# A searched issue order kept as a table, with semaphores between VectorE and GpSimd

## The chip, the cores and the metric

The kernel runs on one core of a Trainium2 chip. The metric is the device time in microseconds (us) of one execution. Most times below are medians of all executions of a kernel; an execution counts as slow when it lies over 1.5% above the fastest of the same kernel, and the ratios and their intervals use the fast ones alone. The span in a profile is the time from the first to the last instruction, 1.7 us less than the metric (190.1 of 191.84 us before).

Engines in the profile: PE is TensorE's matmuls, PEld its weight loads, DVE is VectorE, ACT is ScalarE, POOL is GpSimd, SP is SyncE. Each engine gets its own list of instructions. In the kernel before, ScalarE (198 operations), VectorE (184) and GpSimd (31) start their instructions in the order of the list, so one that waits holds up all that stand behind it; the ScalarE lines further down show a copy of 0.78 us held up by a logarithm that waits 2.11 us for its load.

## The reference

A gated linear attention over 4 batches, 8 heads, 768 steps and head size 48, then an MLP mixer over its output.

```python
# attention
for t in range(S):
    state = alpha[:, :, t, :, None] * state + np.einsum('bhd,bhe->bhde', k[:, :, t], v[:, :, t])
    y[:, :, t] = np.einsum('bhd,bhde->bhe', q[:, :, t], state)
# x = y as (4, 768, 384); token mixing, then channel mixing
h  = np.maximum(x.transpose(0, 2, 1) @ w_tok1, 0.0) @ w_tok2
u  = x + h.transpose(0, 2, 1)
h2 = np.maximum(u @ w_ch1, 0.0) @ w_ch2
out = u + h2
```

## The kernel before

The attention is done in 12 chunks, three to a batch (n = 0 to 11). One chunk takes four loads (`at`, `kt`, `qt`, `vt`, 384 KB each), logarithms and exponentials on ScalarE, elementwise products on VectorE or GpSimd (`pkk`, `pkq`), and small matmuls on parts of the 128x128 array (64*128, 48*128, 64*64 and 48*64 in the trace). The mixer of a batch then has large matmuls of 128x384: token mixing (`t1`, `t2`), transposes (`up`), channel mixing (`c1`, 72 matmuls in 24 groups, each group followed by a relu `rt`; `c2`, 72 matmuls in 24 groups), output adds (`o`) and stores (`st`). Attention of later chunks is laid between the mixer's matmuls of earlier batches.

The program is a list of 838 operations with predecessors, costs and buffer classes. A scheduler written in Python runs while the kernel is being built. It picks the next operation greedily by a cost model and a priority, chooses the engine where there is a choice, and the order that comes out is the order in which each engine gets its instructions:

```python
    def once(self):
        ...
        while avail:
            ...
            for o in avail:
                ...
                for e, (occ, lat) in o.eng.items():          # engines that could do it
                    st = free[e] if free[e] > r else r
                    if e == "PE":
                        ...
                        if o.mode != mode:                   # other array shape
                            st += 95.0
                    elif o.port and port_by != e and port > st and (e == "DVE" or e == "POOL"):
                        st = port                            # model: other engine still in one marked port
                    c = (st, o.pr, st + lat, o, e, occ, lat)
                    if own is None or c[2] < own[2]:
                        own = c                              # earliest finish
                ...                                          # then: earliest start, priority
```

A relu may run on ScalarE or VectorE, and earliest finish sends nearly all of them to ScalarE. A fence (`fe`, a copy of four columns whose result nobody reads; the second half waits for it) on ScalarE or VectorE stands between the two halves `ia` and `ib` of one chunk's attention output:

```python
            ho = ... either(act(384), dve(384)) ...          # relus
        ia = O("ia", pe([48] * 4), 15, ..., mode="R")
        fe = O("fe", either(act(4), dve(4)), 15, reads=[yp], preds=[ia], ...)
        io = O("ib", pe([48] * 4), 15, ..., preds=[fe], mode="R")
```

Both halves of every output tile are stored from SyncE's queue, which also issues all input loads:

```python
    def store(self, o, b, i):
        dst = self.out[b, i * 128 : (i + 1) * 128, :].rearrange("(t s) d -> s t d", s=2)
        for h in range(2):
            self.nc.sync.dma_start(dst[h], self.t(o)[64 * h : 64 * h + 64, :])
```

Of the kernel before, what the change touches and what calls it, by code (L numbers as in the profile page):

```python
# [13 lines left out]
SEM = 50.0  # L14


class Val:
    __slots__ = ("cls", "ops", "buf", "name")

    def __init__(self, cls, name=""):  # L20
        self.cls, self.ops, self.buf, self.name = cls, [], None, name


class Op:
    __slots__ = ("name", "eng", "prio", "preds", "vals", "emit", "mode", "idx",
                 "start", "end", "on", "dma", "port", "pr", "occ", "rdy")

    def __init__(self, name, eng, prio, vals, preds, emit, mode=None, dma=None):
        self.name, self.eng, self.prio = name, eng, prio
        self.vals, self.preds, self.emit = vals, preds, emit  # L30
        self.mode, self.dma = mode, dma
        self.start = self.end = None
        self.on = None
# [31 lines left out]
class Plan:  # L65


    def __init__(self, classes):
        self.classes = dict(classes)
        self.ops = []  # L70
        self.shift = {}
        self.wint = []
# [4 lines left out]
    def op(self, name, eng, prio, writes=(), reads=(), preds=(), emit=None, mode=None, dma=None, port=False):  # L77
        vals = list(writes) + [v for v in reads if v not in writes]
        o = Op(name, eng, prio, vals, list(preds), emit, mode, dma)
        o.port = port  # L80
        for v in vals:
            v.ops.append(o)
        o.idx = len(self.ops)
        self.ops.append(o)
        return o

    def landed(self, s, need):

        t = s
        for a, b in self.wint:  # L90
# [14 lines left out]
    def run(self):  # L105
        self.wint = []
        for _ in range(3):
            self.once()
            w = []
            for a, b in sorted(self.wnew):  # L110
                if w and a <= w[-1][1] + 1.0:
                    w[-1] = (w[-1][0], max(b, w[-1][1]))
                else:
                    w.append((a, b))
            if w == self.wint:
                break
            self.wint = w
        return self.order

    def once(self):  # L120
        free = {e: 700.0 for e in ("PE", "ACT", "DVE", "POOL", "SP")}
        free["POOL"] = free["DVE"] = 3200.0
# [3 lines left out]
        HELD = 1e12  # L126
        bank = [0.0] * 8
        mode = None
        self.wnew = []
        dma_free, dma_w = 2400.0, 0.0  # L130
        warm, wi, acc = False, 0, 0.0
        order, npred, succ, nleft = [], {}, {}, {}
        for o in self.ops:
            o.start = o.end = o.on = None
            o.pr = o.prio + self.shift.get(o.name, 0.0)
            ps = set(o.preds)
            npred[o] = len(ps)
            for p in ps:
                succ.setdefault(p, []).append(o)
            for v in o.vals:  # L140
                nleft[v] = nleft.get(v, 0) + 1
                v.buf = None
        avail = [o for o in self.ops if npred[o] == 0]
        for o in avail:
            o.rdy = 0.0
        relt = {}
        while avail:
            t1 = min(bank)
            t2 = min(max(bank[i], bank[i + 1]) for i in range(0, 8, 2))
            best = None  # L150
            for o in avail:
                r = o.rdy
                for v in o.vals:
                    if v.buf is None:
                        c = v.cls
                        if c == "one":
                            t = t1
                        elif c == "pair":
                            t = t2
                        elif bufs[c]:  # L160
                            t = bufs[c][0][0]
                        else:
                            t = HELD
                        if t > r:
                            r = t
                if r >= HELD:
                    continue
                own = None
                for e, (occ, lat) in o.eng.items():
                    st = free[e] if free[e] > r else r  # L170
                    if e == "PE":
                        if not warm:
                            occ, lat = 2 * occ, 1.5 * lat
                        if o.mode != mode:
                            st += 95.0
                    elif o.port and port_by != e and port > st and (e == "DVE" or e == "POOL"):
                        st = port
                    c = (st, o.pr, st + lat, o, e, occ, lat)
                    if own is None or c[2] < own[2]:
                        own = c  # L180
                if best is None:
                    best = own
                elif own[4] == best[4]:
                    slack = 150.0 if own[4] == "PE" else 60.0
                    if own[1] < best[1]:
                        if own[0] <= best[0] + slack:
                            best = own
                    elif own[0] + slack < best[0] or (own[0] < best[0] and own[1] == best[1]):
                        best = own
                elif own[0] < best[0]:  # L190
                    best = own
            if best is None:
                raise RuntimeError("plan deadlock: " + ", ".join(o.name for o in avail[:30]))
            st, _, _, o, e, occ, lat = best
            o.start, o.on = st, e
            free[e] = st + occ
            self.busy[e] += occ
            o.end = st + lat + SEM
            o.occ = occ
            if o.port and e in ("DVE", "POOL"):  # L200
                port, port_by = st + (lat - 60.0 if e == "DVE" else occ), e
            if e == "PE":
                mode = o.mode
# [11 lines left out]
            if o.dma is not None:  # L215
                kind, dur, lead, tail = o.dma
                if kind == "w":
                    s = max(st + lead, dma_w)
                    dma_w = s + dur
                    self.wnew.append((s, dma_w))  # L220
                    o.end = dma_w + tail
                else:
                    dma_free = self.landed(max(st + lead, dma_free), dur)
                    o.end = dma_free + tail
            for v in o.vals:
                c = v.cls
                if v.buf is None:
                    if c == "one":
                        lim = max(t1, st - 200.0)
                        v.buf = max((i for i in range(8) if bank[i] <= lim), key=lambda i: (bank[i ^ 1], bank[i], -i))  # L230
                        bank[v.buf] = HELD
                    elif c == "pair":
                        lim = max(t2, st - 200.0)
                        v.buf = max((i for i in range(0, 8, 2) if max(bank[i], bank[i + 1]) <= lim),
                                    key=lambda i: (max(bank[i], bank[i + 1]), -i))
                        bank[v.buf] = bank[v.buf + 1] = HELD
                    else:
                        v.buf = bufs[c].pop(0)[1]
                nleft[v] -= 1
                relt[v] = max(relt.get(v, 0.0), o.end)  # L240
                if nleft[v] == 0:
                    if c == "one":
                        bank[v.buf] = relt[v]
                    elif c == "pair":
                        bank[v.buf] = bank[v.buf + 1] = relt[v]
                    else:
                        bufs[c].append((relt[v], v.buf))
                        bufs[c].sort()
            order.append(o)
            avail.remove(o)  # L250
            for s in succ.get(o, ()):
                npred[s] -= 1
                if npred[s] == 0:
                    s.rdy = max(p.end for p in s.preds)
                    avail.append(s)
        if len(order) != len(self.ops):
            raise RuntimeError("not scheduled")
        self.order = sorted(order, key=lambda o: o.start)
        self.span = max(o.end for o in order)


W_SHARE = 0.19
B, H, S, D = 4, 8, 768, 48
HD, DT, DCH = 384, 256, 1536
NB = 3
NS, NM, NDT, NDC = 6, 3, 2, 12
IN_NS, OUT_NS = 1215.0, 560.0
# [11 lines left out]
def build(g):  # L279
# [109 lines left out]
    def weight(nm, piece, npart, bytes_, gate, prio, stage=None):  # L389
        o = P.op(f"ldw_{nm}{piece}", {"POOL": (900.0, 900.0)}, prio, preds=[gate] if gate else [],  # L390
                 writes=[stage] if stage else [], emit=lambda e: g.weight(nm, piece, gate, stage), dma=("w", bytes_ / 285.0, 1600.0, 800.0))
# [3 lines left out]
    def mixer(b):  # L395
# [4 lines left out]
        for m in range(NDT):  # L400
            bank, ht = V("one"), V("ht")
            if b == 0:
                prev = None
                for kc in range(NS):
                    o = P.op(f"t1_{b}_{m}_{kc}", pe([384]), m0 + 900 * m * sc + kc, writes=[bank], reads=[x[kc][0]],
                             preds=[x[kc][1], wl[("wt1", 0)]] + ([prev] if prev else []),
                             emit=lambda e, m=m, kc=kc, bank=bank: g.tok1(bank, m, kc, x[kc][0]))
                    prev = o
            else:
                prev = P.op(f"t1_{b}_{m}", pe([384] * 6), m0 + 900 * m * sc, writes=[bank], reads=[v for v, _ in x],  # L410
                            preds=[o for _, o in x] + [wl[("wt1", 0)]],
# [36 lines left out]
        for i in range(NS):  # L448
# [3 lines left out]
            for q4 in range(4):  # L452
                pp = []
                for mc in range(3 * q4, 3 * q4 + 3):
# [8 lines left out]
            P.op(f"st_{b}_{i}", {"SP": (350.0, 350.0)}, m0 + (16800 + 1950 * (i + 1)) * sc + hold, reads=[o_], preds=[oo],  # L463
                 emit=lambda e, i=i, o_=o_: g.store(o_, b, i), dma=("i", OUT_NS, 1000.0, 700.0))
# [3 lines left out]
    weight("wt1", 0, 1, 786432, gates[NB - 1]["qt"], -70000.0)  # L468
    stage = V("ut")
    weight("wt2", 0, 1, 786432, gates[NB - 1]["qt"], -69990.0, stage)  # L470
# [385 lines left out]
```

## Time and profile before

Median 192.38 us over 3 runs (192.04 to 192.41); span of the profiled run 190.1 us.

Busy times in stretches of the span: each row gives the stretch and its length, then for PE, PEld, DVE, ACT and POOL in this order the busy us and, in brackets, the instructions; then the granted TensorE clock (1 is full; the first event recorded for it in this trace is at 30.4 us, and for the time ahead of that the row prints 1.00 although 128x384 matmuls start 320 ns apart there, twice the 162 of later; whether an event is missing, or the row has no state before the first one, is not shown), the DMA share and GB/s.

```profile
0.00:5.20 5.20, 0.00 (x0) 0.10 (x1) 1.77 (x13) 2.12 (x2) 2.33 (x12) 1.00 0.65 170
5.20:40.90 35.70, 25.01 (x589) 17.65 (x589) 28.01 (x42) 18.34 (x34) 13.20 (x14) 1.00 1.17 248
...
70.00:91.00 21.00, 16.90 (x206) 9.84 (x205) 14.76 (x25) 12.12 (x27) 7.88 (x7) 1.00 0.98 265
91.00:120.00 29.00, 29.00 (x464) 17.78 (x464) 16.80 (x29) 13.69 (x30) 0.42 (x1) 1.00 0.17 40
...
185.10:190.10 5.00, 0.01 (x1) 0.00 (x0) 0.61 (x2) 0.00 (x0) 0.00 (x0) 0.73 0.33 79
```

TensorE is never idle at 91-120, and loses its time in front (10.7 us of idle at 5.2-40.9), at 70-91 (4.1 us) and in a tail of 5.0 us. But a busy TensorE is not a TensorE at its peak: matmuls overlap (a channel matmul is recorded as 333 ns long in the mean, but in an unbroken row the next one starts after 162), and the next lines show where a busy one still loses time. They are the timeline of TensorE (start, duration, matmul group, shape of the array used, operand sizes, count).

```profile
52.44 0.41 PE L673 MATMUL ps<-idn,pkq 64*128 64x64 bf16 x16
52.78 0.66 PE L794 MATMUL ps<-ut,wc 128*128 128x384 bf16 x3
53.37 0.41 PE L673 MATMUL ps<-idn,pkk 64*128 64x64 bf16 x16
53.71 0.44 PE L617 MATMUL ps<-vb,pkk 64*64 64x48 bf16 x32
54.08 1.15 PE L794 MATMUL ps<-ut,wc 128*128 128x384 bf16 x6
```

Three channel matmuls start at 52.78 and the attention matmuls after them at 53.37: 0.59 us for three. Six take from 54.08 to 55.16. At 162 ns from start to start three should take 0.49. The missing 0.1 us is paid each time the array changes shape (128x128, 64x128, 64x64; 48 rows are counted as 64, as a step from 64*128 to 48*128 has a surplus of 10 ns), and here it does so at every one of the four steps. Over this trace, from the first channel matmul on and without longer waits, the mean surplus of a matmul followed by one of another shape is 106 ns (84 of them; 93 to 136 in the mean, by which shape follows which). It is the shape that costs and not the passage to other work: where another group of operands follows on the same shape, the mean surplus is 3 ns on 64x128 (55 such steps) and 12 on 128x128 (57).

Where waits are long, one engine stands in front of work that another needs. ScalarE's timeline ahead of the first channel matmul (start, duration; in brackets: idle time before, and what ended it):

```profile
36.75 0.80 ACT L683 COPY ut<-ps 128x768 bf16<-128x768 bf16 x1 [1.88 <-DVE u L779]
39.65 0.52 ACT L605 ACTIVATE lf<-at 128x384 f32<-128x384 f32 x1 [2.11 <-DMA at<-in_alpha_dram]
40.08 0.78 ACT L683 COPY ut<-ps 128x768 bf16<-128x768 bf16 x1
```

The second `ut` copy, which the first channel matmul at 40.9 needs, stands behind a logarithm of chunk 4 whose load comes late. And VectorE (first two lines) stretches its instructions while GpSimd (last three) runs beside it:

```profile
22.01 1.38 DVE L658 TENSOR_TENSOR pkk<-kt,IE 128x768 bf16<-128x768 f32 x1
23.31 2.22 DVE L658 TENSOR_TENSOR pkq<-qt,E 128x768 bf16<-128x768 f32 x1
...
22.50 1.25 POOL L727 TENSOR_TENSOR ss<-tmp,E 128x192 bf16<-128x192 f32 x1
23.72 0.98 POOL L602 TENSOR_TENSOR at<-at 128x384 f32<-128x384 f32 x1
24.68 1.70 POOL L650 TENSOR_TENSOR kt<-kt,at 128x384 f32<-128x384 f32 x1
```

The same VectorE products take 0.95 us elsewhere in this trace, GpSimd's `ss` 0.50 and `kt` 1.00.

### The profile page before, as it was taken

The numbers are of one execution on the slowest core, as the hardware profiler recorded it, in microseconds if no ns is written. First come the engines' busy times: TensorE is split into PE (matmuls) and PEld (weight loads), VectorE is DVE, ScalarE is ACT, GpSimd is POOL, SyncE is SP. The second block draws the span as 40 slices with busy tenths as digits, with TensorE's granted clock in tenths as the row PEclk, the third lists the DMA queues.
The fourth block names the chain that finished last, engine by engine and source line by source line (L and its number), as shares of the span: only waits on it lengthen the run. The fifth ranks groups of instructions, "written<-read, shape, count | busy, mean of one in ns | idle before, by whom it ended". The sixth has DMA issues, their size and how long they took to land.

```text
span 190.1 us, 5770 instructions
## 1 busy us (share of the span) xinstructions
PE 164.0 (86%) x2489; PEld 101.7 (53%) x2489; DVE 112.8 (59%) x197; ACT 101.2 (53%) x200; POOL 35.9 (19%) x43
## 2 busy tenths in 40 slices
PE   0578578769999988977999999989999999999990
PEld 0357354445566544644566656655656566656650
DVE  3386996993598954869782672894724728100230
ACT  3655536456998624783985212679872121895000
POOL 4023980030431221255200000090000000000000
PEclk9999999978999999999999999999999999999997
DMA  5999999999999998999100123110001132000243
GB/s 156 322 320 270 240 209 207 205 203 270 283 295 247 288 299 229 298 264 269 47 3 3 41 54 75 41 47 5 3 0 40 46 86 71 12 3 0 65 100 83
DMA packets 57625, 27.11 MB, mean 143 GB/s; under 512 B 50816, under 2 KB 57600, under 8 KB 57600
## 3 DMA queue, kind: packets, MB, share of 16 engines
q1 hardware_dynamic: 53760, 23.60, 48.3%
q0 software_dynamic: 3840, 3.15, 10.3%
q8 instruction: 19, 0.31, 0.7%
q14 instruction: 6, 0.05, 0.1%
HBM read 25.17 MB, written 4.72 MB: 157 GB/s over the span
## 4 chain that ended last, share of the span: by engine, by line
PE 62%; DMA 16%; SPq 10%; DVE 6%; ACT 2%; issue 2%; DVEq 0%; ACTq 0%
PE ps L794 26%; PE ps L799 21%; DMA at<-in_alpha_dram 14%; SPq L562 10%; PE ps L617 7%; PE ps L770 3%; DMA out_dram<-o 2%; DVE u L779 2%; PE ps L775 2%; PE ps L673 2%; DVE pkk L658 1%; DVE pkq L658 1%; DVE o L803 1%; PE ps L786 1%; DVE gtm L698 1%
## 5 line engine op out<-in xcount | busy, mean ns | idle before, releaser
L794 PE MATMUL ps<-ut,wc 128*128 128x384 bf16 x288 | 52.8, 333 | 3.3 <-DVE o L803 1.4
L799 PE MATMUL ps<-wc,rt 128*128 128x384 bf16 x288 | 52.5, 327 | 0.0
L765 ACT ACTIVATE rt<-ps 128x384 bf16<-128x384 f32 x93 | 45.1, 490 | 10.9 <-PE ps L794 10.6
L794 PEld LDWEIGHTS <-wc 128*128 128x128 bf16 x288 | 26.9, 99 | 21.5 <-issue 3.7
L799 PEld LDWEIGHTS <-rt 128*128 128x128 bf16 x288 | 26.8, 98 | 17.2
L803 DVE TENSOR_TENSOR o<-ps,u 128x384 f32<-128x384 f32 x24 | 13.1, 555 | 38.1 <-PE ps L799 36.2
L698 DVE TENSOR_TENSOR gtm<-ps,mk 128x1024 bf16<-128x1024 f32 x24 | 28.5, 1218 | 2.3 <-PE ps L617 2.2
L779 DVE TENSOR_TENSOR u<-ps,x 128x384 bf16<-128x384 f32 x24 | 12.7, 552 | 2.0 <-PE ps L775 2.0
L602 POOL TENSOR_TENSOR at<-at 128x384 f32<-128x384 f32 x6 | 6.0, 996 | 33.8 <-DMA at<-in_alpha_dram 22.2
L683 ACT CAST x<-ps 128x384 bf16<-128x384 f32 x16 | 7.2, 479 | 8.1 <-PE ps L617 8.1
L617 PE MATMUL ps<-la,u 128*128 128x384 bf16 x18 | 6.5, 432 | 5.8 <-ACT la L611 5.2
L658 DVE TENSOR_TENSOR pkq<-qt,E 128x768 bf16<-128x768 f32 x10 | 11.0, 1097 | 1.0 <-ACT E L636 1.0
L658 DVE TENSOR_TENSOR pkk<-kt,IE 128x768 bf16<-128x768 f32 x8 | 8.3, 1033 | 4.7 <-ACT IE L642 4.5
L770 PE MATMUL ps<-x,wt 128*128 128x384 bf16 x48 | 10.6, 355 | 0.0
L775 PE MATMUL ps<-ht,wt 128*128 128x384 bf16 x48 | 9.8, 326 | 0.4 <-ACT ht L765 0.4
L673 PE MATMUL ps<-idn,pkk 64*128 64x64 bf16 x192 | 5.5, 202 | 5.4 <-DVE pkk L658 3.1
L617 PE MATMUL ps<-tpq,tpk 48*64 48x128 bf16 x384 | 9.6, 242 | 0.4 <-DVE tpq L685 0.4
L658 POOL TENSOR_TENSOR pkq<-qt,E 128x768 bf16<-128x768 f32 x2 | 3.6, 1810 | 31.8 <-PE ps L673 31.8
L617 PEld LDWEIGHTS <-tpk 48*64 48x64 bf16 x384 | 7.2, 121 | 3.8 <-issue 1.3
L617 PE MATMUL ps<-vb,gtm 64*128 64x48 bf16 x384 | 7.8, 186 | 1.6 <-DVE gtm L698 1.5
L658 POOL TENSOR_TENSOR pkk<-kt,IE 128x768 bf16<-128x768 f32 x4 | 7.2, 1811 | 10.0 <-ACT IE L642 10.0
L765 ACT ACTIVATE ht<-ps 128x384 bf16<-128x384 f32 x7 | 3.4, 490 | 10.5 <-PE ps L770 10.5
(77 smaller groups left out, 194.4 us busy)
## 6 DMA issues: line engine op xcount, KB each, us to landing
at<-in_alpha_dram SPq DMA_DIRECT2D x12, 384.0 KB, 5.3
kt<-in_k_dram SPq DMA_DIRECT2D x12, 384.0 KB, 5.4
qt<-in_q_dram SPq DMA_DIRECT2D x12, 384.0 KB, 5.3
vt<-in_v_dram SPq DMA_DIRECT2D x12, 384.0 KB, 5.2
out_dram<-o SPq DMA_DIRECT2D x48, 96.0 KB, 2.2
wc<-in_moe_w_ch_dram POOLq DMA_DIRECT2D x3, 384.0 KB, 12.6
wc<-in_moe_w_ch_dram POOLq DMA_DIRECT2D x2, 576.0 KB, 16.4
wt<-in_moe_w_tok_dram POOLq DMA_DIRECT2D x2, 192.0 KB, 6.9
```

What stands on the lines that cost most here:

```text
L562: self.ins[id(v)] = self.nc.sync.dma_start(self.t(v), src)
L617: return self.pe.matmul(out, lhsT=lhsT, rhs=rhs, start=start, stop=stop, skip_group_check=True)
L658: self.eng[e].tensor_tensor(self.t(dst)[:, :, :, 0:D], self.t(src).rearrange("p h s d -> p s h d"), bass.AP(tensor=f.tensor, offset=f.offs ...
L673: self.pe.transpose(o[:, c * 64 : c * 64 + 64], s[ph, c % 2, c - c % 2 : c - c % 2 + 2, :], self.idn[ph, ph])
L698: self.nc.vector.tensor_tensor(self.t(gtm)[:, sl, :, :], self.pair(gp).rearrange("p a (j t) -> p (a j) t", t=128), bass.AP(tensor=m.tensor ...
L765: self.act.activation(d, s, AF.Relu)
L770: self.pe.matmul(self.bank(bank)[:, 0:HD], lhsT=self.wt1[:, kc, m * 128 : m * 128 + 128], rhs=self.t(x), start=(kc == 0), stop=(kc == NS - 1))
L775: self.pe.matmul(self.bank(bank)[:, 0:HD], lhsT=self.wt2[:, kc, i * 128 : i * 128 + 128], rhs=self.t(hts[kc]), start=(kc == 0), stop=(kc = ...
L779: self.nc.vector.tensor_tensor(self.t(u), self.bank(bank)[:, 0:HD], self.t(x), ALU.add)
L794: self.pe.matmul(self.bank(bank)[:, 0:HD], lhsT=self.wc1[:, kc, mc * 128 : mc * 128 + 128], rhs=self.t(ut)[:, kc, half * 384 : half * 384 ...
L799: self.pe.matmul(self.bank(bank)[:, 0:HD], lhsT=self.t(rts[mc][0])[:, i * 128 : i * 128 + 128], rhs=self.wc2[:, mc, :], start=(mc == 0), s ...
L803: self.nc.vector.tensor_tensor(self.t(o), self.bank(bank)[:, 0:HD], self.t(u), ALU.add)
```

## The change

The intent: search offline for a better order than the greedy one, keep it as a table, and keep VectorE and GpSimd from stretching each other's instructions as above (2.22 us for a product of 0.95, 1.70 for one of 1.00). The arithmetic and the number of matmuls (2,489) are the same. Cut to its core:

```diff
-    def run(self):            # greedy scheduling at build time
-        ...
+    def run(self, order):     # the table gives order and engine; only buffers are chosen here
+        by = {o.name: o for o in self.ops}
+        self.order = [by[n] for n, _ in order]
+        for n, e in order:
+            by[n].on = e
...
+ENGINES = {"t": "PE", "s": "ACT", "v": "DVE", "g": "POOL", "y": "SP"}
+ORDER = """
+ld_at0y ln0s cumw0t ld_at1y ln1s cumw1t ld_qt0y E0s IE0s ld_at3y qq0g trq0t ld_kt0y kk0v trk0t ln13s ld_qt1y
+ld_vt0y IE1s E1s qq1v ld_kt1y kk1g ld_vt1y evq0v evk0s G0_0t G1_0t Et1s mask0_0v vb0s K0t Et0s mask1_0v trq1t
+...                                                     (839 entries)
+c2_3_0_1t c2_3_0_2t o_2_2v st_2_2y rt_3_0_1s c2_3_5_0t c1_3_7_1t rt_3_9_0v c2_3_0_3t o_3_0v
+...
+c2_3_4_2t c2_3_4_3t o_3_4v st_3_4y
+"""
...
+    def shared(self, i):      # GpSimd and VectorE take turns in operations marked port
+        e, last = self.port_turn, self.port_last
+        if e:
+            if last and last[0] != e:
+                self.tc.add_manual_dep(i.ins, last[1].ins.name, ..., reason="shared port")
+            self.port_last = (e, i)
+        return i
...
-    weight("wt1", 0, 1, 786432, gates[NB - 1]["qt"], -70000.0)
+    for p in range(2):
+        weight("wt1", p, 2, 393216, gates[NB - 1]["kt"], -70000.0 + p)
...
+            last = b == B - 1 and i == NS - 1
...
+        for h, q in enumerate((self.nc.sync, self.nc.scalar if last else self.nc.sync)):
+            q.dma_start(dst[h], self.t(o)[64 * h : 64 * h + 64, :])
```

What the table differs in, counted from it: the loads go in another order (`at` of chunks 3 and 4 early); GpSimd has 40 of the elementwise operations and the permutation of one weight, instead of 23 of them and no permutation; of the 73 operations on VectorE and GpSimd that the code marks `port`, 36 follow one on the other engine and wait for it by a semaphore.

## The prediction

Its sum came to -7.5 us (the middles of its terms add up to -6.6). "Port" in it is the code's word for the operations that take turns; "warm" means the spacing of the matmuls at full clock (162 ns; 320 ahead of 30.4 us).

> **What bounds the kernel now.** Once weights and inputs are there, TensorE bounds it. In the table of stretches PE is busy 29.0 of 29.0 us at 91-120, but 25.0 of 35.7 at 5.2-40.9, 16.9 of 21.0 at 70-91, 5.6 of 6.5 at 120-126.5. Starts of successive matmuls, priced at their warm spacing (162 ns for 128x384), add up to about 135 us of work (estimate); the span is 190.1.
>
> The holes (timeline, list of waits, chain):
> - The first channel matmul starts at 40.9. Its `ut` copy sat on ScalarE behind a logarithm whose `at` load (issued 20.5) landed at 39.6, under the weight transfers.
> - The clock row shows half clock at about 40.6-44.0: about 1.7 us lost.
> - 69.9-72.2: a fence copy on ScalarE sits behind another logarithm waiting for `at` (gap 1.7). 84.9-86.3: an `o` add waits for an output store that queued behind input loads (gap 1.45). At 81 and 89: 1 us more.
> - 122-126: the small attention products and `ut` copies of one batch crowd VectorE: about 1.4 us.
> - Tail: the last two `o` adds end together, four store issues of 0.6 us follow in line on SyncE, and the span ends 5.0 us after the last matmul.
> - Port: while GpSimd ran beside it at 22.5-26.4, VectorE's 128x768 products took 1.38 and 2.22 us (0.95 alone). [...] All such stretching adds up to about 3 us on VectorE, two thirds of it before channel mixing.
>
> **What the change does.** Arithmetic stays the same. Issue order of all engines is a table; loads go in another order (`at` of later chunks ahead, outside the weight transfers), second channel weights later, wt2's permutation to GpSimd, more products on GpSimd (about 40 against 25), semaphores between GpSimd and VectorE [...], the last store split over two queues, the last two groups of outputs finishing about 1.95 us apart.
>
> **Cost and gain on the critical path (estimates from the durations above).**
> - First channel matmul earlier, about 38 instead of 40.9: -2 to -4 us.
> - Half clock avoided perhaps: 0 to -1.7.
> - Gaps at 70-91: -3 of about 4.5.
> - Gaps at 120-126 and 160: -1 of 1.8.
> - Tail: two fewer store issues in line after the last add: -1.2.
> - Semaphore hand-overs (under 0.1 us each, tens of them): +1 to +2; waits where the model behind the table is wrong: +1.
>
> Sum about -7.5 us: 192.4 to 184.8 us. 8 in 10: 181.0 to 189.2. Faster by over 2%: 0.82; within 2%: 0.15; slower: 0.03.
>
> **What would show it.** First channel matmul before 39 us; no ScalarE logarithm waiting for `at` longer than 1 us after 30 us; PE busy at 70-91 over 19 of 21 us; VectorE's 128x768 products all near 0.95 us, GpSimd's near 1.8; 3.8 us from last matmul to end. If the port semaphores matter, VectorE waits before products and copies; I expect little of them after 40 us.
>
> **What would make it wrong.** Loads landing in another order than the table assumes, so that one in-order engine stands in front of work that PE needs (VectorE waiting for GpSimd that waits for a load); weight transfers, issued after GpSimd products that themselves wait for loads, coming late and holding the first token or channel matmuls.

## The result, and the profile after

The changed kernel takes 177.61 us (median of 4 runs, 177.13 to 179.47), against 192.3 us before (median of four, one more than above): a ratio of 0.9256, with a 95% interval of 0.9189 to 0.9322. A ratio is the mean time of one kernel's fast runs over that of the other's of the same rounds, so it is not quite the ratio of the medians. 14.7 us were won and 7.5 were predicted; 177.6 also lies outside the range.

The stretches after (columns as before):

```profile
5.20:38.28 33.08, 25.47 (x601) 18.15 (x600) 22.49 (x36) 19.60 (x35) 16.07 (x17) 1.00 1.17 271
38.28:70.00 31.72, 31.72 (x495) 19.68 (x489) 27.58 (x49) 19.14 (x41) 11.89 (x13) 1.00 1.05 243
70.00:91.00 21.00, 20.54 (x316) 12.95 (x314) 17.88 (x34) 11.97 (x23) 10.77 (x9) 1.00 0.77 204
...
130.00:171.20 41.20, 41.20 (x352) 25.18 (x349) 19.58 (x37) 8.25 (x18) 0.00 (x0) 1.00 0.21 50
171.20:175.40 4.20, 0.00 (x1) 0.00 (x0) 0.56 (x1) 0.00 (x0) 0.00 (x0) 0.88 0.35 84
```

The first channel matmul starts at 38.28 instead of 40.91; at 70-91 TensorE is busy 20.5 of 21 us instead of 16.9; the tail is 4.2 us. TensorE in a stretch of the same kind of work as shown before:

```profile
46.96 0.41 PE L690 MATMUL ps<-idn,pkk 64*128 64x64 bf16 x16
47.20 0.40 PE L690 MATMUL ps<-idn,pkq 64*128 64x64 bf16 x16
47.53 4.07 PE L822 MATMUL ps<-ut,wc 128*128 128x384 bf16 x24
51.54 0.41 PE L690 MATMUL ps<-idn,pkk 64*128 64x64 bf16 x16
51.78 0.40 PE L690 MATMUL ps<-idn,pkq 64*128 64x64 bf16 x16
```

Two attention groups of one array shape now stand next to each other: the second starts 0.24 us after the first (it was 0.34 with a change of shape). Then come 24 channel matmuls in one row, not three. ScalarE before the first channel matmul:

```profile
34.46 0.50 ACT L656 ACTIVATE IE<-ps 128x384 f32<-128x384 f32 x1
34.84 0.54 ACT L622 ACTIVATE lf<-at 128x384 f32<-128x384 f32 x1
35.36 1.01 ACT L711 COPY tpk<-ps 128x1024 bf16<-128x1024 bf16 x1
36.44 1.58 ACT L711 COPY ut<-ps 128x768 bf16<-128x768 bf16 x2
```

The logarithm of chunk 4 stands at 34.84 and finds its load there: no wait. VectorE's products by group (busy us, mean ns, idle before), first before, then after:

```profile
L658 DVE TENSOR_TENSOR pkq<-qt,E 128x768 bf16<-128x768 f32 x10 | 11.0, 1097 | 1.0 <-ACT E L636 1.0
L658 DVE TENSOR_TENSOR pkk<-kt,IE 128x768 bf16<-128x768 f32 x8 | 8.3, 1033 | 4.7 <-ACT IE L642 4.5 <-ACT IE L639 0.2
```

```profile
L675 DVE TENSOR_TENSOR pkk<-kt,IE 128x768 bf16<-128x768 f32 x8 | 7.6, 955 | 6.6 <-POOL pkq L675 6.4
L675 DVE TENSOR_TENSOR pkq<-qt,E 128x768 bf16<-128x768 f32 x5 | 4.8, 953 | 0.0
```

No product is stretched any more. VectorE's first one is said to wait 6.4 us for GpSimd's turn, but the turn is not what cost that time: without the semaphores the same product waits 6.1 us for its own load (e1b below).

### Where the 14.7 us are, by an account of TensorE's starts

I priced every matmul at the usual distance from its start to the next one's start (the mean over the full-clock part of the trace before, without the lowest tenth and the highest fifth, by kind: 162 ns for 128x384). What a distance has above its price is surplus. The account is an estimate from the two traces:

| us | before | after | gain |
|---|---|---|---|
| until the first matmul | 5.2 | 5.2 | 0.0 |
| priced matmuls, all | 134.1 | 134.1 | 0.0 |
| surplus before the first channel matmul | 23.5 | 20.2 | 3.3 |
| after it: in the stretch at half clock | 1.5 | 0.0 | 1.5 |
| after it: in gaps over 0.25 us each | 6.5 | 1.9 | 4.6 |
| after it: in smaller surpluses | 14.0 | 9.5 | 4.5 |
| after the last matmul | 5.0 | 4.2 | 0.8 |

(The rows add up to within 0.3 us of the spans; the last matmul's own length is missing.) The row that I had not looked at is the last but one. Of its 4.5 us, 3.2 are changes of shape: after the first channel matmul there are 88 of them before and 55 after; those with less than 0.25 us of surplus sum to 8.9 us (84 of them, 106 ns each) and 5.8 us (55, 105 ns each). This row is also the steadiest: 9.3 to 9.5 us in all five profiles of the new table with nothing taken from it (the change, a0, e8, e8b, e12), and 12.6 to 14.0 in three of the old order (before, e2, e3). The gaps are not steady: 1.9 to 5.3 us in the same five.

### The profile page after: what moved, and what is told of

Same layout as the page of the kernel before. It is cut to its first block, busy times and chain, and to the rows that moved or that the text cites. A ratio compares the mean times of both kernels' runs of the same rounds, so it can differ in the third digit from the quotient of the medians.

```text
span 175.4 us, 5752 instructions
## 1 busy us (share of the span) xinstructions
PE 157.1 (90%) x2489; PEld 100.4 (57%) x2489; DVE 122.3 (70%) x224; ACT 78.7 (45%) x154; POOL 52.9 (30%) x62
## 4 chain that ended last, share of the span: by engine, by line
PE 69%; DMA 12%; SPq 9%; DVE 3%; issue 2%; POOL 2%; ACT 1%; DVEq 0%; POOLq 0%
PE ps L827 25%; PE ps L822 21%; PE ps L634 8%; SPq L581 8%; PE ps L798 5%; PE ps L803 5%; DMA wt<-in_moe_w_tok_dram 4%; DMA qt<-in_q_dram 3%; DMA at<-in_alpha_dram 3%; PE ps L814 2%; PE ps L690 2%; DMA out_dram<-o 2%; SPq L614 2%; DVE o L831 1%; DVE rt L795 1%
## 5 line engine op out<-in xcount | busy, mean ns | idle before, releaser
L822 PE MATMUL ps<-ut,wc 128*128 128x384 bf16 x288 | 51.3, 326 | 0.1
L827 PEld LDWEIGHTS <-rt 128*128 128x128 bf16 x288 | 26.8, 98 | 16.9
L793 ACT ACTIVATE rt<-ps 128x384 bf16<-128x384 f32 x48 | 22.1, 491 | 28.7 <-PE ps L822 25.5
L795 DVE TENSOR_SCALAR rt<-ps 128x384 bf16<-128x384 f32 x48 | 24.9, 551 | 9.1 <-PE ps L822 8.9
L675 POOL TENSOR_TENSOR pkq<-qt,E 128x768 bf16<-128x768 f32 x7 | 12.7, 1813 | 8.3 <-ACT E L659 4.8
L754 POOL TENSOR_TENSOR ss<-tmp,E 128x192 bf16<-128x192 f32 x9 | 4.6, 508 | 32.1 <-DVE tmp L751 31.0
L807 DVE TENSOR_TENSOR u<-ps,x 128x384 bf16<-128x384 f32 x24 | 11.9, 550 | 2.3 <-PE ps L803 2.1
L675 DVE TENSOR_TENSOR pkk<-kt,IE 128x768 bf16<-128x768 f32 x8 | 7.6, 955 | 6.6 <-POOL pkq L675 6.4
L711 ACT COPY ut<-ps 128x768 bf16<-128x768 bf16 x6 | 4.8, 798 | 11.3 <-PE ps L814 11.2
L711 ACT CAST x<-ps 128x384 bf16<-128x384 f32 x12 | 5.7, 483 | 8.9 <-PE ps L634 8.9
L711 ACT COPY tpk<-ps 128x1024 bf16<-128x1024 bf16 x7 | 7.1, 1014 | 2.7 <-PE ps L690 2.7
```

Source lines behind the costliest of these rows:

```text
L675: self.shared(self.eng[e].tensor_tensor(self.t(dst)[:, :, :, 0:D], self.t(src).rearrange("p h s d -> p s h d"), bass.AP(tensor=f.tensor, o ...
L711: return self.act.copy(d, s)
L793: self.act.activation(d, s, AF.Relu)
L795: self.nc.vector.tensor_scalar_max(d, s, 0.0)
L822: self.pe.matmul(self.bank(bank)[:, 0:HD], lhsT=self.wc1[:, kc, mc * 128 : mc * 128 + 128], rhs=self.t(ut)[:, kc, half * 384 : half * 384 ...
L827: self.pe.matmul(self.bank(bank)[:, 0:HD], lhsT=self.t(rts[mc][0])[:, i * 128 : i * 128 + 128], rhs=self.wc2[:, mc, :], start=(mc == 0), s ...
```

## The experiments

Theory A: the table carries the gain, by fewer long waits and by fewer changes of array shape. Rivals: B, the semaphores between VectorE and GpSimd carry a good part (products took 1.38 and 2.22 us beside GpSimd in the trace before, 0.95 elsewhere); C, changes of shape hide in waits anyway, and only the long holes counted; D, the even split of the relus counts. The old order could be written down as a table too (each operation and the engine that the greedy scheduler had given it), so the two orders can be tried in the same machinery. Ratios are against the kernel before, run in the same rounds.

| run | order | other edit | median us | ratio, 95% interval |
|---|---|---|---|---|
| change | new | none | 177.61 | 0.9256 (0.9189 to 0.9322) |
| a0_after | new | none | 178.99 | 0.9286 (0.9233 to 0.9339) |
| e1_after_no_sem | new | no semaphores | 179.84 | 0.9368 (0.9274 to 0.9463) |
| e1b_no_sem | new | the same again | 180.03 | 0.9362 (0.9318 to 0.9407) |
| e2_before_order_sem | old | all else as changed | 193.68 | 1.0076 (0.9979 to 1.0172) |
| e3_before_order_plain | old | no semaphores, one store queue | 192.71 | 1.0082 (0.9984 to 1.018) |
| e4_ungrouped | new, 88 changes of shape | none | 181.22 | 0.944 (0.936 to 0.952) |
| e6_relu_act | new | all relus on ScalarE | 182.39 | 0.9488 (0.9424 to 0.9553) |
| e7_load_order | new, old order of 20 loads | none | 191.05 | 0.9965 (0.9902 to 1.0028) |
| e5_holes | old, three holes mended | as e3 | 191.55 | 0.9943 (0.9858 to 1.0027) |
| e9_before_relu_split | old | as e3, half the relus on VectorE | 196.26 | 1.0147 (1.006 to 1.0234) |
| e10_before_grouped | old, 60 changes of shape | as e3 | 196.57 | 1.0239 (1.0145 to 1.0332) |
| e8_split_right_store | new | split on the last store | 177.7 | 0.9265 (0.9219 to 0.931) |
| e8b_split_again | new | the same again | 177.74 | 0.922 (0.9148 to 0.9291) |
| e12_more_o | new | the same, five output buffers | 177.35 | 0.9191 (0.9125 to 0.9258) |

All gave correct results. a0, e1b, e8 and e6 ran on one chip, e1 to e4 on another, e5 and e7, and later e9, e10, e12 and e8b, on a third. The medians hold slow runs too: a0's, 1.4 us over what was expected, has two slow ones among six. Its four fast runs lay between 177.25 and 179.49 us, with a median of 178.0, so 1 us is about what one run can differ by.

### e1 and e1b: the semaphores alone

```diff
-            g.port_turn = o.on if o.port and o.on in ("DVE", "POOL") else None
+            g.port_turn = None
```

> The changed kernel without the semaphores between VectorE and GpSimd, same table. Theory A (the table carries the gain, by fewer holes and fewer changes of array shape on TensorE): within 1 us of 177.6. Rival B (the semaphores carry a good part, [...]): 179.6 us or more, with VectorE's 128x768 products stretched past 1.3 us again in several places.

> The changed kernel once more, unedited, as the measure for the runs beside it on the same chip. Both theories: 177.6 us, within 0.8.

> The same kernel as e1_after_no_sem, now beside the unedited change on one chip. If the 2 us of e1 are the semaphores' (rival B in part), it is 1.5 to 3 us over a0_after again; if they came from the chip or from chance, within 0.7 us of it.

Measured: 2.2 us more than the change by the ratios in e1 (0.9368 less 0.9256, times 192.3), 1.5 us more in e1b beside a0. Both times the mean is higher, but the intervals of each pair overlap, so I take 1 to 2 us as likely and not as settled. What the semaphores prevent shows plainly in the trace of e1b:

```profile
L672 DVE TENSOR_TENSOR pkk<-kt,IE 128x768 bf16<-128x768 f32 x8 | 9.2, 1145 | 6.3 <-DMA kt<-in_k_dram 6.1
L672 DVE TENSOR_TENSOR pkq<-qt,E 128x768 bf16<-128x768 f32 x5 | 6.1, 1229 | 0.3 <-DMA qt<-in_q_dram 0.2
```

Mean 1145 and 1229 ns, against 955 and 953 with semaphores; single products take up to 2.3 us. Not every VectorE instruction is stretched: in the trace before, a mask (`gtm`, one input in PSUM) took 1.22 us from 89.58 on beside GpSimd's product of 1.81 us at 89.60, and the mean of all 24 masks is 1.22. What decides between the two was not tried. So theory A keeps most of the gain, but its forecast for e1 (within 1 us of 177.6) was missed, and the semaphores are probably worth something in this order.

### e2 and e3: the old order in the new machinery

```diff
 ORDER = """
-ld_at0y ln0s cumw0t ld_at1y ln1s ...                    (the searched table)
+ld_at0y ld_kt0y ld_qt0y ld_vt0y ld_at1y ld_kt1y ...     (what the greedy scheduler gave)
```

and in e3 also `g.port_turn = None` and both store halves on SyncE's queue.

> The order of the kernel before, written out as a table in the changed kernel: semaphores, the split last store, and weight loads waiting for the k load as changed. Theory A: 190 to 193 us. Rival B: 189 us or less, as the semaphores alone then win 3 us.

> Control: the same order, no semaphores, last store on one queue; only the table form, bank choice and the load that the weights wait for differ from the kernel before. Both theories: 191 to 193.5 us. If it is far from 192.3, the rest of the rewrite matters and e2 must be read against this run.

e3 is within 1% of the kernel before: the table form, the bank choice and the gate of the weight loads carry nothing visible. e2 is no faster than e3. In the old order, which gives GpSimd less, the semaphores show no gain, and not the 3 us that rival B asked for; rival B falls as the main cause. (A gain of a us or two could be hidden: e2's profile holds two stretches at half clock, 3.6 us of surplus, and e3's one, 1.7 us.)

### e4: more changes of shape, everything else kept

19 channel matmul groups moved among TensorE's work. Two of the places, with TensorE's entries alone:

```diff
-trk4t trq4t c1_0_5_1t c1_0_4_0t
+trk4t c1_0_5_1t trq4t c1_0_4_0t
...
-G1_8t K8t G0_8t c2_1_1_0t c2_1_1_1t c2_1_1_2t
+G1_8t c2_1_1_0t K8t c2_1_1_1t G0_8t c2_1_1_2t
```

All other engines keep their order, and the attention groups theirs among themselves.

> The changed table with 19 channel matmul groups moved by one to four places among TensorE's work, so that after the first channel matmul the array changes shape 88 times, as in the kernel before, and not 55. Theory A: 33 changes at the 105 ns that a change costs in both traces is 3.5 us more: 181.1 us (180.3 to 182.2). Rival C (such changes hide in waits that are there anyway; the gain came from the long holes alone): 178.6 us or less.

Measured 181.22 us, 3.6 us over the change (3.5 by the ratios; 3.0 against a0). The account of its trace agrees for the term in question: 88 changes of shape after the first channel matmul at 105 ns, 9.2 us in place of 5.8. (The gaps over 0.25 us are 0.6 us there and 1.9 in the change, so the two profiled spans differ by 2.3 us only; the gaps vary that much between profiles of one kernel.) A piece of it:

```profile
52.04 0.41 PE L687 MATMUL ps<-idn,pkk 64*128 64x64 bf16 x16
52.38 0.66 PE L819 MATMUL ps<-ut,wc 128*128 128x384 bf16 x3
52.97 0.41 PE L687 MATMUL ps<-idn,pkq 64*128 64x64 bf16 x16
```

Where the change has 0.24 us between the two transposing groups and channel matmuls in a row, here each step takes 0.34 or 0.59 again. Rival C falls: on a TensorE that is otherwise full, as here, the changes of shape are paid nearly or wholly in full.

### e10: the reverse, fewer changes in the old order

```diff
-c1_1_9_0t c1_1_9_1t y7t ia7t c1_1_10_0t ib7t c1_1_10_1t
+c1_1_10_0t c1_1_9_0t c1_1_9_1t y7t ia7t ib7t c1_1_10_1t
```

(TensorE's entries alone; one place of many.)

> The order of the kernel before (as e3_before_order_plain), its attention matmuls grouped by moving channel matmuls out from between them by up to four places, so that the array changes shape 60 times after the first channel matmul and not 88. If changes of shape can be saved without anything else, 28 at 105 ns are 2.9 us less than e3: about 189.8 us. If the moved matmuls had been covering waits of the attention chain, the saving is given back as longer waits before attention matmuls: 192 us or more.

Measured 196.57 us, slower than the kernel before beyond the interval, and 3 us over e3 by the ratios (those intervals overlap slightly, and the two ran on different chips). The 2.9 us that were to be won are in any case not there. The changes were saved (the surpluses under 0.25 us fell from 13.0 to 10.7 us), and more than given back: the gaps over 0.25 us rose from 8.4 to 14.2 us. Nine of them, of 0.42 to 0.49 us, stand between the two halves `ia` and `ib` of a chunk: the moved channel matmuls had been covering the fence copy there. One of them, in TensorE's timeline of e10 (the two halves are the groups of eight that read `ss`; in brackets the idle time before and what ended it, here the fence):

```profile
59.51 0.26 PE L631 MATMUL ps<-ss,tpq 48*128 48x48 bf16 x8
60.10 0.27 PE L631 MATMUL ps<-ss,tpq 48*128 48x48 bf16 x8 [0.33 <-DVE junkDVE L709]
```

In the new table other work stands between the halves as well, often attention of another chunk, which needs no change of shape or only one. So I take it that grouping is a gain only if enough attention work is ready at once; one way of grouping was tried.

### e6 and e9: the split of the relus

```diff
-rt_0_0_1v rt_0_9_1v ... (48 relus on VectorE)
+rt_0_0_1s rt_0_9_1s ... (all 96 on ScalarE)
```

> All 96 channel relus on ScalarE (before: 93 of 96; changed: 48 and 48). ScalarE's busy time goes from 79 to about 101 us, VectorE's from 122 to about 96. Theory A (TensorE hardly waits for relus in either kernel): within 1 us of a0_after. Rival D (the even split of the relus carries part of the gain): 2 us or more above it.

Measured 182.39 us; by the ratios 3.9 us over a0 on the same chip, and the intervals do not overlap. TensorE now waits for ScalarE's relus, in the list of waits (engine and line, what it waited for: us in sum, times, longest):

```profile
PE ps L631 <- ACT rt L790: 1.6, 4, 0.6
```

No such wait for ScalarE stands in the list of the change. All gaps over 0.25 us after the first channel matmul are 5.8 us in e6; four profiles of the new table with its split (the change, a0, e8, e8b) have 1.9, 5.3, 2.6 and 2.8. So the rest of the 3.9 us is not traced to single waits. ScalarE's relus in e6, as a group:

```profile
L790 ACT ACTIVATE rt<-ps 128x384 bf16<-128x384 f32 x96 | 41.8, 514 | 21.0 <-PE ps L819 20.4
```

ScalarE sat idle for 21 us in sum before these relus: an engine with much idle time still makes others late. Rival D holds for the new order. The reverse in the old order:

> The order of the kernel before (as e3_before_order_plain), with 49 of its 96 channel relus, those of every second half, given to VectorE without moving anything. If an even split is worth 3 us by itself (as e6 could be read), 189.5 us or less. If it pays only in an order made for it, 192 us or more: VectorE has the attention work to do in the same stretches.

Measured 196.26 us: no gain; it is slower than the kernel before beyond the interval, and 1.3 us over e3 by the ratios (those intervals overlap). Where the time goes I can only argue, that VectorE has relus in front of masks which TensorE waits for; its one profile fell on a slow run. (In it TensorE waits 4.4 us for masks after 40 us, against 2.5 in e3, which fits.) Of these two orders, only the new one gains by an even split.

### e7: the loads in the old order under the new table

```diff
-ld_at0y ld_at1y ld_qt0y ld_at3y ld_kt0y ld_qt1y ld_vt0y ld_kt1y ...   (SyncE's entries alone)
+ld_at0y ld_kt0y ld_qt0y ld_vt0y ld_at1y ld_kt1y ld_qt1y ld_vt1y ...
```

> The changed table with the first 20 loads issued chunk by chunk as in the kernel before; every other engine's own order is kept. Theory A' (queue order and load order work only together): GpSimd stands at the product for chunk 4, whose load is now 17th, in front of all weight loads, and the first channel matmul comes 5 us or more later: 182 us or more. Rival (load order matters little, the loads are ahead anyway): 179 us or less.

Measured 191.05 us. All of the gain is gone by changing the places of loads that move the same bytes. The first channel matmul starts at 50.3 us: of the 15.1 us by which its profiled span is longer than that of the change, 12.0 are surplus before that matmul. GpSimd's issue of the first weights is late as expected (33.97 instead of 19.67), but the first stop is another one than I had named. ScalarE stands at the logarithm of chunk 3, whose `at` load has gone from 4th to 13th place, in front of the exponentials of chunk 1:

```profile
18.91 0.52 ACT L619 ACTIVATE lf<-at 128x384 f32<-128x384 f32 x1 [7.45 <-DMA at<-in_alpha_dram]
19.34 0.79 ACT L656 ACTIVATE IE<-ps 128x768 f32<-128x768 f32 x1
```

This does not say that the new load order is worth 13 us in itself. It says that the order of a queue and the order of each engine are one thing.

### e5: mending the three longest holes of the old order by hand

```diff
-... trq3t s0_3v up_0_1t evq3v P4g ln14s ut_0_1s ... lnP4s mask0_3v c1_0_0_0t r14s ...
+... trq3t s0_3v up_0_1t evq3v P4g ut_0_1s ... rt_0_2_0s ln14s lnP4s r14s ...
-... st_0_2y P9v ln19s ia5t c2_0_3_3t fe5s r19s ib5t c2_0_4_2t x0_5s x1_5v ...
+... st_0_2y ia5t c2_0_3_3t fe5s ib5t c2_0_4_2t x0_5s ln19s r19s x1_5v P9v ...
-    "x": 14, "ht": 4, "u": 13, "ut": 2, "rt": 24, "o": 3,
+    "x": 12, "ht": 4, "u": 11, "ut": 2, "rt": 24, "o": 5,
```

> The order of the kernel before (as e3_before_order_plain: no semaphores, one queue), with its three longest holes mended by hand: the logarithms of chunk 4 moved behind the ut copies and first relus on ScalarE, those of chunk 9 (and VectorE's product for it) behind the fence and the x copies, five output buffers instead of three (two x and two u buffers given up for the room). If holes can be taken away one by one, 3 to 6 us less than e3_before_order_plain, so 187 to 190 us. If the wait only moves to the next late thing, 191 us or more.

Measured 191.55 us, 1.2 us under e3 by the medians (2.7 by the ratios, whose intervals overlap). The gap at 70 us is gone and the one at 85 us shrank from 2.6 to 1.0 us. But the first channel matmul still starts at 40.95, now after a new gap of 2.65 us at 35.3, and a new gap of 1.84 us stands at 90.0, beside a VectorE product of 0.55 us that takes 1.89 there. Most of what was mended came back as the next late thing.

### e8, e8b and e12: a try at a faster version

The change splits the store of tile 5 of the last batch over two queues, but its table ends with tile 4. In its trace the ScalarE queue issues at 166.47, and the last two issues, at 171.82 and 172.34, are both SyncE's.

```diff
-            last = b == B - 1 and i == NS - 1
+            last = b == B - 1 and i == NS - 2
```

> The change splits the store of output tile 5 of the last batch over two queues, but its table finishes tile 4 last. Here the split goes to tile 4. If the end of the span follows the last store's issue, it is 0.3 to 0.8 us under a0_after (one issue of 0.59 us out of the line); if not, no difference.

> The measure for e12_more_o on the same chip: e8_split_right_store once more, 177.7 us within 0.8.

e12 has this edit and the line of buffer counts from e5:

> A try at a version better than both: the change with the split on the store that is last, and five output buffers instead of three (two x and two u buffers given up). In both traces of the unedited change VectorE waits about 3 us for stores, and TensorE 0.8 to 1.5 us of that near 100 us. If those waits go, 0.7 to 1.5 us under e8b_split_again: about 176.6 us; if VectorE is late there anyway, no difference.

By the traces, the tail after the last matmul goes from 4.2 to 4.0 us with the split in the right place; the times cannot tell it (0.9265 beside 0.9286). e12 takes the waits for output buffers away: VectorE's 2.7 us of them in e8b are not in its trace. Its fast runs are the fastest measured, 175.98 to 177.65 us with a ratio of 0.9191, but the interval overlaps that of e8b. It is at best half a microsecond better, and that is not settled.

## Why the prediction was wrong

Direction and most mechanisms were right; the size was off by a factor of two. Two steps failed: a cost was entered that did not come (5), and, the larger one, a gain was left out because only visible holes were summed (6). Term by term:

1. *"First channel matmul earlier, about 38 instead of 40.9: -2 to -4 us."* Right: 38.28, and 0.6 us more of priced work done before it, 3.3 us together. No logarithm waits for `at` in front of it any more.
2. *"Half clock avoided perhaps: 0 to -1.7."* 1.5 us in this pair of profiles: before, the clock row has 0.50 at 40.6-44.0, and 128x384 matmuls start 320 ns apart there. It is not a stable term: other profiles of the old order have the half clock elsewhere (e3 from 89.1 us, e2 from 64.9 and 88.8), each time after or at the end of a gap of 2.4 to 2.6 us; the profiles of the changed kernel and of e8, e8b and e12 have it only ahead of channel mixing or after the end.
3. *"Gaps at 70-91: -3 of about 4.5"* and *"Gaps at 120-126 and 160: -1 of 1.8."* -4.0 predicted, -4.6 for all gaps over 0.25 us in this pair of profiles. That fit is partly luck: the changed kernel's profile is of its fastest run; in a0's, of a run of 179.5 us, such gaps are 5.3 us and not 1.9, and the term would be -1.2. What I had not seen is that such gaps could not have been taken away one by one (e5).
4. *"Tail: two fewer store issues in line after the last add: -1.2."* Measured -0.8 (before, the last four issues on SyncE take 0.47 to 0.59 us each). Only the spacing of the last two tiles worked; the split was read off the diff without looking up which store is last in the table.
5. **The first step that failed:** *"Semaphore hand-overs (under 0.1 us each, tens of them): +1 to +2; waits where the model behind the table is wrong: +1."* This entered 2 to 3 us of cost. The time of one hand-over was about right: in the trace before, engines that waited for an instruction of another mostly started 0.03 to 0.09 us after its end (VectorE's product at 7.72, 0.03 us after ScalarE's `IE`; TensorE at 8.73, 0.06 after that product; GpSimd's product at 12.96, 0.08 after `IE`). In the trace of the change 12 of the 36 turns are what ended a wait, and the second engine started 0.03 to 0.18 us after the first. But no such cost is to be seen in sum: the semaphores look like a gain of 1 to 2 us in the new order (e1, e1b), not a loss. Of the waits, all gaps over 0.25 us, wrong guesses of the model included, are 1.9 us in sum in the profile of the change, but up to 5.3 in others, so the 1 us entered for them cannot be judged.
6. **The second step that failed, a term that was missing:** the small surpluses, 4.5 us. *"Starts of successive matmuls, priced at their warm spacing ..., add up to about 135 us of work (estimate); the span is 190.1"*: I had that difference and then, under *"The holes"*, summed only those that can be seen as holes. 88 changes of array shape at 106 ns stood in the trace before, and the new table could be counted before any run: 55. e4 shows that such changes are paid there, 3.0 to 3.6 us for 33 of them.
7. Not costed either: the relus, 93 and 3 before, 48 and 48 in the table. Without that split the new order loses 3.9 us (e6). That gain is part of the rows above (it shows as gaps), not one to be added to them.

The middles of my terms add up to -6.6 us (I wrote -7.5). Without the 2.5 us of cost in step 5 they would be -9.1, and with the small surpluses of step 6 -13.6; the remaining 1.1 us of the measured 14.7 are small errors of steps 1 to 4. What stays open is how the gain divides between causes: grouping or the relu split alone, in the one way that each was tried, do not make the old order faster (e10, e9), and the new order without either loses 3 to 4 us (e4, e6). They are gains only inside the new order, so no single share can be given to each. Not tested alone is the move of 17 products and of a weight's permutation to GpSimd.

What the prediction named as signs came out so: the first channel matmul before 39 us, yes; no logarithm waiting over 1 us after 30 us, no: one waits 3.36 us at 57.6, but TensorE is busy all through that stretch, and none waits where the first channel matmul hangs on it; TensorE busy over 19 of 21 us at 70-91, yes (20.5); products near 0.95 us, yes; 3.8 us of tail, no (4.2).

## What to carry to other kernels

Count, in a trace and in a proposed order, how often TensorE changes its array shape, and price each change as a wait; on an otherwise full TensorE nearly all of it was paid here (e4: 3.0 to 3.6 us for 33 changes, at 105 ns each). When several in-order engines and a load queue feed one another, treat their orders as one object: single improvements that are right in themselves (fewer changes of shape in e10, a better balance in e9, earlier copies in e5) can lose or win little until the rest is arranged around them. An engine's idle time in sum doesn't mean that it may take more work (e6: ScalarE idle for 21 us in sum before its relus, and 3.9 us lost): ask what stands behind that work in its queue.
